# Gated linear attention and a top-2 expert router on one core: three leading experts instead of four, and one unit's routing moved into the attention chunks

## The chip, the cores and the metric

One core of a Trainium2 chip runs the whole program. The metric is device time in microseconds of one execution, as the median of repeated runs. The core has five engines that run their own instruction queues in order: PE (matrix products), DVE (vector work), ACT (scalar work, activations), POOL (here mainly indirect DMAs, which read or write rows by an index list) and SP (here plain DMAs and DMA transposes). They wait for each other through semaphores.

## The reference, cut to what matters

```python
# attention: batch 4, 8 heads, 768 steps, head width 48
state = np.zeros((B, H, D, D))
for t in range(S):
    state = alpha[:, :, t, :, None] * state + np.einsum('bhd,bhe->bhde', k[:, :, t], v[:, :, t])
    y[:, :, t] = np.einsum('bhd,bhde->bhe', q[:, :, t], state)
x = y.transpose(0, 2, 1, 3).reshape(3072, 384)
# router: 8 experts, hidden width 1024, two experts for a row
logits = x @ w_gate
noisy_logits = logits + np.log1p(np.exp(x @ w_noise)) * noise
top2 = np.argpartition(-noisy_logits, 2, axis=1)[:, :2]
top2_w = softmax of the two chosen logits
for e in range(8):
    for k in range(2):
        mask = top2[:, k] == e
        h = np.maximum(x[mask] @ w1[e], 0.0)
        out[mask] += top2_w[mask, k, None] * (h @ w2[e])
```

Everything is float32.

## The kernel before, in words

**Attention.** The 3,072 rows are worked on as 24 chunks of 128 (six chunks for a batch element). Within a loop step `n` PE transposes the inputs of chunks `n+2` and `n+3`, makes the output of chunk `n`, the state and the scores of chunk `n+1`, and brings the output of chunk `n-1` back to rows (`rows_of`, L277). DVE makes running products (two scans, L373 and L385), scales the queries (`q_P`, L413), adds the state (`S`, L472) and copies the scores under a mask (L445). The masked scores of a chunk are read by the product L254 of that chunk's output. The score tiles have one buffer each. The order of the pieces within a step is a list of names (`ORDER`, for the last but one step `LATE_ORDER`).

**Routing.** Six chunks make a unit; there are four units. `routing(u, on)` is a generator: logits, `Exp`, `Ln` on ACT (with loads of ACT's function tables), the best two of eight on DVE two chunks at a time (L742, L743), gates, ranks by two small matmuls (L795, L796), and the place of each row in a `table` in DRAM by expert. It leaves 12 indirect DMAs for each unit ("puts", L173) that POOL issues later, one or a few at a time (`put_some`). The units 0 and 1 are routed beside later attention chunks, at the steps and places of `ROUTE`; the units 2 and 3 beside the expert pairs, at the times in `beside()`. In the attention steps unit `u`'s pieces stand at `n - (u + 1) * UC + 1`, so they begin one step behind the unit's last chunk.

**Expert pairs.** The chosen rows are worked on in 24 pairs, each 256 rows of one expert, then three small tiles for what is left. A pair needs a list from the table (`tab`), its index list (`find_rows`, DVE), the gathered rows (`x_in`, POOL, L1008), their transposes, and the sums of weights and rows of a fast matrix scheme (DVE). `THIRD` is 4: pairs 0 to 3 are the first 256 rows of experts 0 to 3, pairs 4 to 15 three pairs each of experts 4 to 7, pairs 16 to 23 two each of experts 3 to 0. Pairs 0 and 1 have their layers one behind the other; from pair 2 on, the second layer of a pair lies between the steps of the next pair's first layer. Below `DEEP` (= `THIRD`) the first layer has 11 steps of four 128x128 products (`product1`, L1348), from `DEEP` on 10 (`step1`, L1356). The second layer has 7 steps (`product2`, L1363). Every matmul shows as two records, so a step has eight.

**Order.** Every step of a pair has a time on a plan in which pair `i` begins at `20 * i`; all steps are sorted by it and recorded in that order, and each engine runs its own in that order. The outputs of a pair go through one of two buffers (`os[i % 2]`, L1377 and L1381) and are written and added to `out` by indirect DMAs on POOL (L992 and L1000). `PUT_LATER` delays those of pairs 1 to 4 on the plan. ACT scales the first half of pair `i` into the buffer that pair `i-2` used, so it waits until that pair's DMAs have landed. A put of the table is also made to wait for the DVE sum that stands before it on the plan.

## Time and profile before

| | |
|---|---|
| median of 3 runs | 620.96 us (620.77 to 621.24) |
| the profiled execution | 621.97 us, of which the span from the first to the last instruction is 620.3 us |
| PE busy | 607.0 us, 98% of the span |
| DVE busy | 508.0 us, 82% |
| ACT busy | 330.9 us, 53% |
| POOL busy | 317.4 us, 51% |
| attention, to the first product of pair 0 | 0 to 153.7 us |
| pairs and small tiles on PE | 153.7 to 612.5 us |
| granted clock of PE | 0.997 of full speed |

PE is busy nearly all of the time, so a saving of work on another engine shows only where PE waits for it. Where PE waits, the view of waits names the engine and the line that ended the wait, and the timeline (instructions in order of time, with the idle time before each) shows when.

### The profile page before, as it was taken

What the parts mean: (1) busy time and instruction counts of PE and PEld (TensorE: products, weight loads), DVE (VectorE), ACT (ScalarE), POOL (GpSimd) and SP (SyncE); (2) the same over time, 40 slices, a digit from 0 to 9 for tenths busy, and PEclk for the clock granted to TensorE, in tenths of its full rate; (3) what the DMA queues carried; (4) which work ended last, traced back from release to release, by engine and by line L of the source; (5) the groups of instructions that cost most, each with busy time, mean ns of one, the idle gap of its engine ahead of it and who ended that gap; (6) DMA issues with size and microseconds to landing.
All of it is one profiled execution on the core that took longest, in us unless ns stands there. A gap on an engine that the chain in (4) does not pass through costs nothing.

```text
span 620.3 us, 14271 instructions
## 1 busy us (share of the span) xinstructions
PE 607.0 (98%) x5274; PEld 583.7 (94%) x5274; DVE 508.0 (82%) x1158; ACT 330.9 (53%) x665; POOL 317.4 (51%) x355
## 2 busy tenths in 40 slices
PE   8999999999999999999999999999999999999994
PEld 5899999999999999999999999999999999989894
DVE  8788898988879869968898798887688879878672
ACT  4877868685655334444444544445544445444431
POOL 7353267884137786545434434555347527443254
PEclk9999999999999999999999999999999999999998
DMA  9999999984997854664654837775997678885223
GB/s 144 175 199 223 237 188 175 214 179 106 259 235 145 235 136 128 126 166 121 115 126 105 171 66 200 193 98 132 271 211 199 140 184 221 181 220 118 80 44 55
DMA packets 181552, 101.09 MB, mean 163 GB/s; under 512 B 150088, under 2 KB 172074, under 8 KB 181472
## 3 DMA queue, kind: packets, MB, share of 16 engines
q1 hardware_dynamic: 145056, 35.56, 34.5%
q10 hardware_dynamic: 21280, 44.05, 24.4%
q0 software_dynamic: 15136, 20.47, 14.8%
q8 instruction: 44, 0.72, 0.5%
q14 instruction: 36, 0.29, 0.2%
HBM read 76.41 MB, written 24.22 MB: 162 GB/s over the span
## 4 chain that ended last, share of the span: by engine, by line
PE 81%; DVE 6%; POOL 5%; issue 4%; ACT 2%; DMA 1%; POOLq 0%; ACTq 0%; DVEq 0%
PE sc L1356 19%; PE h_ps L1363 18%; PE o_ps L1363 13%; PE c_ps L1356 8%; PE sc L1348 4%; PE tp L345 3%; PE sc L425 3%; PE y L254 2%; PE h_ps L277 2%; POOL table L173 2%; PE y L493 2%; DVE P_all L373 1%; POOL k_P L403 1%; PE tp L452 1%; PE h_half_ps L1678 1%
## 5 line engine op out<-in xcount | busy, mean ns | idle before, releaser
L992 POOL DMA_INDIRECT out_dram<-o,where x46 | 48.5, 1054 | 166.6 <-DVE o L1381 91.1
L1367 ACT ACTIVATE h<-h 128x512 f32<-128x512 f32 x92 | 56.9, 628 | 78.2 <-DVE h L1229 61.7
L1000 POOL DMA_INDIRECT out_dram<-o,where x44 | 71.0, 1615 | 13.4 <-issue 13.1
L1008 POOL DMA_INDIRECT x_in<-x_rows,where x48 | 58.6, 1220 | 24.4 <-issue 12.7
L1363 PE MATMUL o_ps<-wt,hx 128*128 128x192 f32 x384 | 70.8, 327 | 0.0
L1356 PE MATMUL sc<-yT,ws 128*128 128x128 f32 x480 | 66.6, 275 | 1.5 <-DVE m L1232 1.5
L1356 PEld LDWEIGHTS sc<-yT,ws 128*128 128x128 f32 x480 | 62.9, 191 | 1.8 <-DVE m L1232 1.8
L173 POOL DMA_INDIRECT table<-entry,place_u x48 | 55.0, 1145 | 16.5 <-issue 9.5
L1363 PEld LDWEIGHTS o_ps<-wt,hx 128*128 128x128 f32 x384 | 61.5, 190 | 1.8 <-issue 1.8
L403 POOL TENSOR_TENSOR k_P<-k_P,over 128x512 f32<-128x512 f32 (+1 forms) x24 | 27.7, 1154 | 40.5 <-DVE over L385 32.3
L1223 ACT COPY xt<-x_turned 128x768 uint16<-128x768 uint16 x44 | 43.8, 1053 | 2.1 <-DMA x_turned<-x_in 2.1
L345 PE MATMUL tp<-ident,ins 128*128 128x128 f32 x288 | 42.9, 282 | 1.6 <-ACT k_P L395 0.6
L1377 ACT ACTIVATE o<-h_ps,tab 128x192 f32<-128x192 f32 x46 | 19.4, 421 | 42.7 <-PE h_ps L1363 41.3
L345 PEld LDWEIGHTS tp<-ident,ins 128*128 128x128 f32 x288 | 32.1, 144 | 7.1 <-ACT k_P L395 1.0
L445 DVE COPY_PREDICATED shared<-upto,sc 128x512 f32<-128x512 uint32 x47 | 32.0, 736 | 7.6 <-PE sc L425 7.0
L1488 ACT COPY m<-sc 128x512 f32<-128x512 f32 x20 | 11.7, 586 | 48.0 <-PE sc L1356 48.0
L1363 PE MATMUL h_ps<-wt,h 128*128 128x192 f32 x192 | 35.2, 327 | 0.0
L1363 PE MATMUL o_ps<-w,h 128*128 128x192 f32 x192 | 35.2, 326 | 0.0
L1363 PE MATMUL h_ps<-wt,hx 128*128 128x192 f32 x192 | 35.2, 326 | 0.0
L1363 PE MATMUL h_ps<-w,h 128*128 128x192 f32 x192 | 35.1, 326 | 0.0
L1363 PE MATMUL h_ps<-w,hx 128*128 128x192 f32 x192 | 35.1, 326 | 0.0
L1356 PE MATMUL c_ps<-xs,w 128*128 128x128 f32 x240 | 33.3, 275 | 0.0
(333 smaller groups left out, 1611.9 us busy)
## 6 DMA issues: line engine op xcount, KB each, us to landing
w<-in_moe_w_dram ACTq DMA_DIRECT2D x33, 512.0 KB
w<-in_moe_w_dram ACTq DMA_DIRECT2D x44, 384.0 KB
ins<-in_alpha_dram SPq DMA_DIRECT2D x24, 192.0 KB
ins<-in_k_dram SPq DMA_DIRECT2D x24, 192.0 KB
ins<-in_q_dram SPq DMA_DIRECT2D x24, 192.0 KB
vt<-in_v_dram SPq DMA_DIRECT2D x24, 192.0 KB
x_rows<-y_sb SPq DMA_DIRECT2D x24, 192.0 KB
ins<-in_moe_w_dram ACTq DMA_DIRECT2D x9, 512.0 KB
```

The costliest lines, as they stand in the source:

```text
L173: put = nc.gpsimd.indirect_dma_start(out=table, out_offset=bass.IndirectOffsetOnAxis(ap=place, axis=0), in_=entry, in_offset=None, bounds_ ...
L345: nc.tensor.transpose(tp[:, j, :], src[:, 2 * j:2 * j + 2, :], ident)
L403: (nc.vector if n == NT - 1 else nc.gpsimd).tensor_tensor(c["k"][:, at], c["k"][:, at], over[:, at, 1:CB], op=ALU.mult)
L445: nc.vector.copy_predicated(MTs[n % 2][:, i], mask_upto, sc)
L992: put = nc.gpsimd.indirect_dma_start(out=out, out_offset=bass.IndirectOffsetOnAxis(ap=at, axis=0), in_=rows, in_offset=None, bounds_check= ...
L1000: add = nc.gpsimd.indirect_dma_start(out=out, out_offset=bass.IndirectOffsetOnAxis(ap=at, axis=0), in_=rows, in_offset=None, bounds_check= ...
L1008: nc.gpsimd.indirect_dma_start(out=rows, out_offset=None, in_=x_rows[0:units * UT, :], in_offset=bass.IndirectOffsetOnAxis(ap=at, axis=0), ...
L1223: nc.scalar.copy(halves[:, part], x_turned[:, :, part].rearrange("p s a t -> p s (a t)"))
L1348: nc.tensor.matmul(bank[name][:, f, :], W[:, ds(f * C, C)], X, start=new and f == 0, stop=True, skip_group_check=True)
L1356: nc.tensor.matmul(bank[name][:, 2 * h + f, :], W[h][:, ds(f * C, C)], X[h], start=new and not h and not f, stop=True, skip_group_check=True)
L1363: nc.tensor.matmul(bank[name], H[:, f, :], W[:, f, :], start=new and f == 0, stop=True, skip_group_check=True)
L1367: nc.scalar.activation(t, t if src is None else src, AF.Relu)
```

## The change

It changes numbers in the plan, and three conditions in the routing.

- `THIRD` becomes 3. Pairs 0 to 2 are the first rows of three experts, pairs 3 to 17 are five experts of three pairs each, pairs 18 to 23 two each of the first three. `DEEP` follows, so pair 3 has the 10-step first layer; the weights of an expert are loaded 11 times instead of 12.
- Unit 2 is routed at the steps `n` = 18 to 21 of the attention loop, by a third row of `ROUTE` that repeats the row of unit 1. Its rank and the check of expert lists (`check_third`, L859) use PSUM of the pool that the attention's rows use. Four of its puts stand in the attention loop, eight in pair 0.
- Unit 3 takes the times that unit 2 had in `beside()`, and its puts stand in pairs 1 and 2. The steps of the plan that follow from all lists (`route_on(3)` after the puts, `out_of_range`) come one pair sooner.
- `PUT_LATER` is empty: the outputs of pairs 1 to 4 are no longer delayed on the plan.
- The small tiles 0 and 1 begin at pairs 18 and 20 instead of 16 and 18; the third stays at 22.

```diff
-    AFTER_GROUP = (4, 5, 7)
-    THIRD = E - 4
+    AFTER_GROUP = (5, 6, 7)
+    THIRD = E - 5
...
-            for u in range(2):
+            for u in range(NU - 1):
                 for _ in range(ROUTE[u].count((n - (u + 1) * UC + 1, place))):
                     next(routes[u], None)
...
-            if (u, c) in ((NU - 2, 2), (NU - 1, 0)):
+            if (u, c) == (NU - 1, 0):
                 nc.scalar.activation(unread_exp, ones[0:1, 0:1], AF.Exp)
...
-        if u < NU - 2:
+        if u < NU - 1:
             nc.scalar.activation(unread_exp, ones[0:1, 0:1], AF.Exp)
...
-        rank = few(on, [C, UC, E], "rank", u >= NU - 2)
+        rank = few(on, [C, UC, E], "rank", u >= NU - 1)
...
-    DEEP, BY_DMA = THIRD, THIRD - 2
+    DEEP, BY_DMA = THIRD, THIRD - 1
...
-        PUT_LATER = {1: 13.0, 2: 16.0, 3: 12.0, 4: 6.0}
+        PUT_LATER = {}
...
-            left += [(t, lambda: route_on(2)) for t in when((0, 8.95), (0, 12.0), ...
-            left += [(t, lambda: route_on(3)) for t in when((1, 5.0), (1, 10.2), ...
+            left += [(t, lambda: route_on(3)) for t in when((0, 8.95), (0, 12.0), ...
```

Where instructions then stand:

DVE in loop step 20, between the scaled queries of chunk 22 (`q_P`) and the masked scores of chunk 21. Before:

```order
L413 TENSOR_TENSOR q_P<-tp,P_all 128x512
L472 TENSOR_TENSOR S_156<-S_155,o_ps 128x192
L445 COPY_PREDICATED shared<-upto,sc_2352 128x512
L445 COPY_PREDICATED shared<-upto,sc_2353 128x512
L1182 TENSOR_SCALAR tab_2279<-tab_2279 128x2
```

Now (the two chunks of `top` and `at` that stand behind `q_P` here stand twice more in the rows above it):

```order
L413 TENSOR_TENSOR q_P<-tp,P_all 128x512
L742 MAX top<-noisy 128x8
L743 MAX_INDEX at<-top,noisy 128x8
...
L749 CAST at_f<-at 128x6x2
L754 TENSOR_TENSOR entry<-top 128x12
L766 TENSOR_TENSOR den<-entry 128x6
...
L783 TENSOR_TENSOR counts<-picked 128x6x8
L788 SCALAR_TENSOR_TENSOR past<-within,counts 128x56
L472 TENSOR_TENSOR S_156<-S_155,o_ps 128x192
L445 COPY_PREDICATED shared<-upto,sc_2396 128x512
L445 COPY_PREDICATED shared<-upto,sc_2397 128x512
```

Unit 2's choice of experts now stands ahead of the state and the masked scores of chunk 21; `den` waits for ACT's gates.

ACT in loop step 19, between the state block of chunk 19 and the output `yT` of that chunk. Before:

```order
L454 COPY k_end<-tp 128x512
L415 COPY P_end<-P_all 128x4
L479 COPY S_block<-S 64x4x48 x2
L496 COPY yT<-y 128x512
L363 ACTIVATE ins,above<-ins,less 128x8x48
```

Now:

```order
L479 COPY S_block<-S 64x4x48 x2
L689 ACT_TABLE_LOAD
L689 ACTIVATE noisy<-noisy 128x48
L496 COPY yT<-y 128x512
L363 ACTIVATE ins,above<-ins,less 128x8x48
```

A load of the function table and the `Ln` of unit 2 now stand between them; DVE's next instruction of unit 2 needs that `Ln`.

POOL from the gather of pair 4 to the outputs of pair 1. Before:

```order
L1008 DMA x_in<-x_rows,where_2781 128x768 x2
L173 DMA table<-entry,place_u 25600x8
L753 MEMSET entry 128x12x4
...
L173 DMA table<-entry,place_u 25600x8 x6
L1008 DMA x_in<-x_rows,where_3175 128x768 x2
...
L992 DMA out_dram<-o_186,where_2463 3072x384
L1000 DMA out_dram<-o_186,where_2463 3072x384
```

Now:

```order
L1008 DMA x_in<-x_rows,where_3051 128x768 x2
L173 DMA table<-entry,place_u 25600x8 x2
L992 DMA out_dram<-o_186,where_2520 3072x384
L1000 DMA out_dram<-o_186,where_2520 3072x384
...
L1155 DMA tab_3225<-table 128x6x8
L1008 DMA x_in<-x_rows,where_3279 128x768 x2
```

Two table puts stand ahead of the outputs of pair 1 there, where nine and the gather of pair 5 stood.

## Rows read from the trace of the kernel before

**Rows 1.** Waits of PE: engine, line, waited for, total us, times, longest.

```profile
PE sc L1356 <- DVE m L1232: 1.5, 1, 1.5
PE tp L345 <- DVE q_P L413: 0.4, 2, 0.2
```

**Rows 2.** Windows, pairs 0 to 3: length, then busy us of PE, PEld, DVE, ACT, POOL.

```profile
152.20:224.00 71.80, 71.80 (x573) 71.49 (x574) 61.55 (x188) 38.94 (x70) 37.70 (x45) 1.00 0.87 215
```

**Rows 3.** Timeline, DVE, unit 1's routing: start, duration, line, op, [idle before <-releaser].

```profile
97.24 0.21 DVE L737 TENSOR_TENSOR noisy<-noisy,noise 128x48 f32<-128x48 f32 x1
...
97.95 1.36 DVE L445 COPY_PREDICATED shared<-upto,sc 128x512 f32<-128x512 uint32 x2 [0.19 <-PE sc L425]
...
99.89 1.21 DVE L373 TENSOR_TENSOR_SCAN P_all<-shared,least 128x516 f32<-128x516 f32 x1
...
104.57 0.28 DVE L749 CAST at_f<-at 128x12 f32<-128x12 uint32 x1
...
106.76 0.33 DVE L472 TENSOR_TENSOR S<-S,o_ps 128x192 f32<-128x192 f32 x1
```

**Rows 4.** Timeline, ACT: unit 1's `Ln`, and the state block of chunk 19.

```profile
95.67 1.28 ACT L689 ACT_TABLE_LOAD   x1
96.97 0.24 ACT L689 ACTIVATE noisy<-noisy 128x48 f32<-128x48 f32 x1
...
134.09 0.71 ACT L479 COPY S_block<-S 64x192 f32<-64x192 f32 x2 [1.70 <-POOL S L473]
```

**Rows 5.** Timeline, DVE, chunks 20 to 23 of the attention.

```profile
135.54 1.37 DVE L445 COPY_PREDICATED shared<-upto,sc 128x512 f32<-128x512 uint32 x2 [0.62 <-issue]
136.79 2.02 DVE L373 TENSOR_TENSOR_SCAN P_all<-shared,least 128x516 f32<-128x516 f32 x1
...
141.37 0.35 DVE L472 TENSOR_TENSOR S<-S,o_ps 128x192 f32<-128x192 f32 x1 [0.43 <-PE o_ps L467]
142.35 1.35 DVE L445 COPY_PREDICATED shared<-upto,sc 128x512 f32<-128x512 uint32 x2 [0.62 <-PE sc L425]
...
149.12 0.68 DVE L413 TENSOR_TENSOR q_P<-tp,P_all 128x512 f32<-128x512 f32 x1
```

**Rows 6.** Timeline, DVE, the places of unit 2's rows and what follows.

```profile
180.46 0.26 DVE L801 TENSOR_TENSOR picked<-picked,rank 128x96 f32<-128x96 f32 x1
...
181.56 0.25 DVE L722 TENSOR_TENSOR lg<-lgs 128x96 f32<-128x96 f32 x1
```

**Rows 7.** Timeline, PE: chunk 22's output; the rank of unit 3 and what follows.

```profile
149.98 1.09 PE L254 MATMUL y<-shared,vt 128*48 128x128 f32 x16
...
201.99 0.34 PE L795 MATMUL rank<-counts,before 128*128 128x48 f32 x2
...
202.37 1.53 PE L1363 MATMUL o_ps<-wt,hx 128*128 128x192 f32 x8
```

**Rows 8.** Timeline, PE: second layers of pairs 3 and 4, then two later pairs.

```profile
225.97 1.47 PE L1363 MATMUL o_ps<-w,h 128*128 128x192 f32 x8
...
246.28 1.47 PE L1363 MATMUL o_ps<-w,h 128*128 128x192 f32 x8
...
390.10 0.61 PE L1356 MATMUL sc<-xt,w 128*128 128x128 f32 x4
...
390.99 1.47 PE L1363 MATMUL o_ps<-w,h 128*128 128x192 f32 x8
...
409.02 1.47 PE L1363 MATMUL o_ps<-w,h 128*128 128x192 f32 x8
```

**Rows 9.** Timeline, ACT: pair 3's first half scaled into its output buffer.

```profile
230.97 0.42 ACT L1377 ACTIVATE o<-o_ps,tab 128x192 f32<-128x192 f32 x1 [3.86 <-DMA out_dram<-o,where]
```

**Rows 10.** Timeline, SP and ACT: the DMA transposes of pair 2, and their readers.

```profile
165.37 2.82 SPq L1212 DMA_TRANSPOSE x_turned<-x_in  x2
...
178.75 1.06 ACT L1223 COPY xt<-x_turned 128x768 uint16<-128x768 uint16 x1
...
455.92 1.07 ACT L1223 COPY xt<-x_turned 128x768 uint16<-128x768 uint16 x1 [2.12 <-DMA x_turned<-x_in]
```

## What the change was predicted to do

> **What bounds the kernel now.** I read the page first: PE is busy for 98% of the span, so the time is PE's own work plus its few waits. Then the waits of PE, by line. The longest that belong to this change's neighbourhood are small: one of 1.5 us for a sum of weights, and two of 0.2 us in the attention chunks, one behind the routing of unit 0 and one behind that of unit 1 [rows 1]. The windows say the same of the first four pairs: PE busy 71.80 us of 71.80, DVE only 61.55 [rows 2]. So DVE, ACT and POOL may be relieved in these pairs without any gain; only PE's work counts, and what makes PE wait. The timelines then give four places: the last attention chunks, where DVE is full [rows 5]; the few PE instructions that vanish [rows 7, 8]; one wait on ACT for outputs [rows 9]; and the DMA transposes of pair 2 [rows 10].
>
> **Part 1, unit 2's routing in the attention chunks: +4.0 us.** The masked scores of chunk 22 must stand before PE can make that chunk's output. On DVE they end when `q_P` of the next chunk starts, at 149.12 [rows 5]; PE begins the output at 149.98 [rows 7], 0.86 later, after work of its own. So there is 0.86 us of slack at that place, and what DVE loses above it PE waits for.
>
> What DVE gets to do between chunks 20 and 23 is priced by what unit 1 took, and by unit 2's own rows in the pairs.
> - Start: ACT's state block of chunk 19 begins at 134.09 and takes 0.71 [rows 4]. Behind it stand the table load and the `Ln`. For unit 1 the `Ln` began 1.30 after the load (95.67 to 96.97) and took 0.24 [rows 4]. So the noisy logits can begin on DVE at 134.09 + 0.71 + 1.30 + 0.24 = 136.34, where DVE before began its masked copy at 135.54 [rows 5]: 0.80 late.
> - Two operations that finish the noisy logits: 97.24 to 97.95 less the wait of 0.19, 0.52 [rows 3].
> - `top` and `at` for six chunks, two at a time: from 97.95 to 99.89 a masked copy and one pair of chunks lie, 1.94 [rows 3]; the copy alone is 1.25 (135.54 to 136.79) [rows 5], so 0.69 for two chunks, 2.07 for six.
> - Gates and counts: 104.57 to 106.76, 2.19 [rows 3].
> - Places from the rank: 180.46 to 181.56, 1.10 [rows 6].
>
> Together 0.52 + 2.07 + 2.19 + 1.10 = 5.88, and 0.80 for the start. Against it go waits in which DVE now has work: 0.43 and 0.62 [rows 5], and the scan of 2.02 [rows 5], which took 1.21 beside unit 1 [rows 3]: I estimate that it does so again, since POOL's vector work, which ran beside it, stands elsewhere now; 0.81. That is 1.86 in all. `q_P` of chunk 23 starts at 149.12 + 0.80 + 5.88 - 1.86 = 153.94, and PE's output of chunk 22 at about 154.0 instead of 149.98: **+4.0**. All that stands behind moves with it, pair 0 too. If the scan stays at 2.02 it is 4.8; if the late start is covered by the first wait, 3.2. The rank's matmuls and ACT's gates lie within this stretch of DVE and are not counted again. The puts that POOL issues here hide behind the chunks, as those of unit 1 did; without that cover, a put would hold only the gathers, which are rival 2.
>
> What this relieves in the pairs, DVE's routing of unit 2, is worth nothing there, since PE did not wait [rows 2].
>
> **Part 2, PE's own work in the pairs.** The rank of a unit takes PE from 201.99 to 202.37, 0.38 [rows 7]. Unit 2's now lies in the attention, where PE waits for DVE anyway: **-0.38**. Pair 3 loses one step of four products; a step lasts 0.89 (390.10 to 390.99) [rows 8]: **-0.89**. The one load of an expert's weights that is saved, with its sums on DVE, hides behind PE now (PE has no idle time there [rows 2]): 0. The most it could be worth is the one wait for such a sum, 1.5 [rows 1], which lies elsewhere and has pairs in front of it that stay as they are.
>
> **Part 3, outputs of pair 1.** ACT waits 3.86 us before it can scale pair 3's first half, for the DMAs that write pair 1's outputs [rows 9]. PE feels it: from the second layer of pair 3 to that of pair 4 it takes 20.31 us (225.97 to 246.28), where a regular pair takes 18.03 (390.99 to 409.02) [rows 8]. The difference is 2.28. In the new order two table puts stand ahead of these outputs on POOL, where nine and a gather stood, so they go out well before they are needed: **-2.28**. What is late next in the pair is PE itself, as in the regular pairs.
>
> **Part 4, the rest: 0.** Unit 3's routing and its puts take the times that unit 2's had, with the same distance to the lists that need them and with DVE less filled. The small tiles and the plan's other steps come a pair or two sooner with the same instructions; their cover is PE at 71.80 of 71.80 [rows 2], and a small tile that came too soon would cost about the wait that such a piece has now, 1.5 [rows 1].
>
> **The sum.** 4.0 - 0.38 - 0.89 - 2.28 = +0.45 us on the profiled execution of 621.97, so 622.42. That execution lies 1.01 above the median of 620.96, so I add the 0.45 to the median: **621.4 us**. With the ends of part 1 (3.2 and 4.8) its own range is 620.6 to 622.2.
>
> **Rival 1, faster: DVE has room.** Units 0 and 1 were routed the same way, and PE waited 0.2 us behind each [rows 1]. If unit 2's work also fits into DVE's gaps, only the 0.80 of the late `Ln` stays, and the sum is 0.80 - 0.38 - 0.89 - 2.28 = -2.75: 618.2. For it speaks that the operations are the same. Against it, that around chunk 20 to 22 DVE's own waits are only 0.43 and 0.62 [rows 5], too few for 5.88, and that for unit 1 there were many more chunks left over which PE could fall behind and catch up, while behind unit 2 stand three. Chance 0.15.
>
> **Rival 2, slower: the transposes of pair 2 come late.** Pair 2's rows are gathered by POOL, and SP turns them by DMA (issued 165.37 for 2.82; ACT reads them at 178.75) [rows 10]. Between gathers and outputs POOL has seven more items there than before: unit 2's puts in pair 0 and more. From the end of the second issue (168.19) to the reader there are 10.6 us. Both ends move by about 4.0 with part 1, but the issue by about 1 more for the puts. The one reader in the trace that had to wait for such a transpose waited 2.12 [rows 10]. If it happens to pair 2, ACT's queue stands, and PE behind it: 0.45 + 2.12 = 2.57, so 623.5. It decides from a landing later than about 9.5 us after the second issue. Against it, no other reader of the trace waits so. Chance 0.13.
>
> **Rival 3, the change does not do what it says.** POOL's outputs of pair 1 now stand ahead of the puts of unit 3, but they come only when the pair's results do, and if the DMAs in front (gathers, puts with their waits) still hold POOL, ACT's wait of rows 9 stays and the 2.28 are not gained: 623.7. [Rows 9] show only that the outputs landed late, not which item held them. Chance 0.08.
>
> **Rival 4, the table load costs more than its row.** In this trace the `Ln` begins 1.30 after the load starts, and the load lasts 1.28 [rows 4]; nothing else lies between. Were the load followed by as long again, 1.28, before the `Ln` could run, DVE's chain would start 1.3 later and the time would be 622.7. The rows of unit 1 show no such gap, so its chance is 0.04. The Trainium skill ("ScalarE: Activation LUTs", section "What ACT_TABLE_LOAD costs") says that a switch costs a drain of about 1380 ns beside the load of about 1283 ns; by that figure, an estimate from the page, the sum would be about 622.8. The load agrees with the trace, the drain does not show in it.
>
> **How the numbers follow.** Forecast 0.60, rivals 0.15, 0.13, 0.08, 0.04. About 0.2%, 619.7 to 622.2, is what a measurement of this kernel can tell from no change. Of the forecast's 0.60 I put 0.48 within its own range, which lies within that bound, 0.02 below it and 0.10 above, since the terms I left at 0 in part 4 are more likely to cost than to gain. Faster: 0.15 + 0.02 = 0.17. Same: 0.48. Slower: 0.10 + 0.13 + 0.08 + 0.04 = 0.35. The range goes from 619.5 to 623.9: it takes in the forecast and rivals 2 to 4 and leaves out rival 1 (0.15) and what lies beyond 623.9, some 0.04.
>
> **What would show it.** Part 1: the first product of pair 0 at about 157.7 instead of 153.7; DVE with hardly an idle moment from 136.3 to `q_P` of chunk 23; PE waiting for DVE in the chunks 21 to 23. If pair 0 starts before 155.5, rival 1 has it. Part 2: pair 3 in steps of L1356, and no rank between the layers of pairs 0 to 2 but unit 3's. Part 3: no wait for `out_dram` at L1377, and some 18 us from pair 3's second layer to pair 4's. Rival 2: a wait for `x_turned` at L1223 in pair 2. Rival 4: the `Ln` 2.6 instead of 1.3 behind its load. The prediction is wrong if PE has new idle time in pairs 0 to 5, or if the shift of pair 0 lies outside 3.2 to 4.8.

## The result: slower by 1.1%, and the profile after

The changed kernel takes 627.96 us in the median of 6 executions (623.91 to 632.24), the kernel before 620.99 (6 executions, 620.40 to 621.63). The ratio is 1.0109, with a 95% interval of 1.0067 to 1.0151, so some 7 us more. The forecast was 621.4, the range 619.5 to 623.9: the time lies outside it. Two things are new: the shift of the pairs is larger than forecast, and the times scatter over 8 us, where the kernel before stays within 1.3. In some runs below the kernel before took 630 to 633 us as well; there only the difference to it counts.

The profiled execution took 628.84 us, 6.87 more than that of before. It is one of six that lie 8 us apart, so the table shows where this execution lost its time, and not where each of them did. It is read from PE's timeline: for each pair the start of its second layer, and its distance to the one before it.

| stretch on PE | before, us | after, us | difference |
|---|---|---|---|
| start to pair 0's first product | 153.69 | 159.23 | +5.54 |
| to pair 0's second layer | 13.50 | 14.32 | +0.82 |
| to that of pair 1 | 19.37 | 23.68 | +4.31 |
| to that of pair 2 | 20.49 | 19.82 | -0.67 |
| to that of pair 3 | 18.93 | 18.03 | -0.90 |
| to that of pair 4 | 20.31 | 18.26 | -2.05 |
| to that of pair 13 | 162.74 | 162.52 | -0.22 |
| to that of pair 20 | 134.22 | 135.59 | +1.37 |
| to PE's end | 69.28 | 69.28 | 0.00 |
| from PE's end to the span's end | 7.80 | 6.50 | -1.30 |

The span grows from 620.3 to 627.2. The table's rows sum to 6.9.

PE's waits in the changed kernel, as [rows 1] show them for before (engine, line, what was waited for, us in total, times, longest):

```profile
PE sc L1348 <- ACT m L1423: 2.4, 1, 2.4
PE h_ps L277 <- ACT yT L496: 1.4, 2, 1.0
...
PE h_ps L795 <- DVE counts L783: 1.3, 1, 1.3
PE sc L1356 <- ACT m L1496: 0.6, 1, 0.6
```

The first is in pair 1 and the last in pair 18; the two in the middle are in the attention's end. The one wait of 1.5 us in [rows 1] is gone, and these took its place.

**The attention's end.** DVE's timeline, which answers [rows 5] (start, duration, line, [idle before]):

```profile
136.45 1.39 DVE L737 TENSOR_TENSOR noisy<-noisy,noise 128x48 f32<-128x48 f32 x1 [1.48 <-ACT noisy L689]
137.87 0.42 DVE L738 TENSOR_TENSOR noisy<-noisy,lg 128x48 f32<-128x48 f32 x1
138.22 1.35 DVE L445 COPY_PREDICATED shared<-upto,sc 128x512 f32<-128x512 uint32 x2
...
140.14 1.21 DVE L373 TENSOR_TENSOR_SCAN P_all<-shared,least 128x516 f32<-128x516 f32 x1
...
144.89 0.18 DVE L749 CAST at_f<-at 128x12 f32<-128x12 uint32 x1
...
147.33 0.33 DVE L472 TENSOR_TENSOR S<-S,o_ps 128x192 f32<-128x192 f32 x1
...
155.44 0.68 DVE L413 TENSOR_TENSOR q_P<-tp,P_all 128x512 f32<-128x512 f32 x1
```

`q_P` of chunk 23 starts at 155.44, forecast was 153.94, before 149.12. The `Ln` is not to blame: its load and itself on ACT, then the POOL product beside DVE's first row, and the same product before the change, where it stood beside the scan of 2.02 in [rows 5]:

```profile
134.88 1.28 ACT L689 ACT_TABLE_LOAD   x1
136.17 0.24 ACT L689 ACTIVATE noisy<-noisy 128x48 f32<-128x48 f32 x1
```

```profile
136.57 1.20 POOL L403 TENSOR_TENSOR k_P<-k_P,over 128x512 f32<-128x512 f32 x1
```

```profile
136.50 1.21 POOL L403 TENSOR_TENSOR k_P<-k_P,over 128x512 f32<-128x512 f32 x1
```

PE in the same place, then in pair 1:

```profile
147.09 0.62 PE L795 MATMUL h_ps<-counts,before 128*128 128x48 f32 x2 [1.27 <-DVE counts L783]
...
147.94 2.03 PE L493 MATMUL y<-q_P,S_block 128*128 128x128 f32 x8
...
155.37 1.25 PE L254 MATMUL y<-shared,vt 128*48 128x128 f32 x16
...
159.23 1.07 PE L1348 MATMUL sc<-xt,w 128*128 128x128 f32 x8
...
186.61 1.12 PE L1348 MATMUL sc<-xt,ws 128*128 128x128 f32 x8
190.14 1.16 PE L1348 MATMUL sc<-xs,ws 128*128 128x128 f32 x8 [2.41 <-ACT m L1423]
191.13 1.55 PE L1348 MATMUL sc<-xt,w 128*128 128x128 f32 x8
192.48 1.91 PE L1348 MATMUL c_ps<-xt,w 128*128 128x128 f32 x8
...
197.23 1.47 PE L1363 MATMUL o_ps<-w,h 128*128 128x192 f32 x8
```

The output of chunk 22 is at 155.37 (forecast 154.0, before 149.98 in [rows 7]). A product that takes 1.06 elsewhere takes 2.03 at 147.94 and up to 1.91 behind the wait of pair 1. The windows say why (length, then busy us of PE, PEld, DVE, ACT and POOL, the granted clock, the busy share of the DMA engines and GB/s):

```profile
148.00:149.00 1.00, 1.00 (x6) 1.00 (x6) 0.96 (x4) 0.70 (x2) 0.25 (x1) 0.50 0.52 183
192.00:193.00 1.00, 1.00 (x7) 1.00 (x6) 0.21 (x1) 0.00 (x0) 0.65 (x1) 0.50 1.05 389
```

A granted clock of 0.50 is the 1.2 GHz level. It stands behind both of PE's longer idle stretches (1.02 and 1.27 us close together, and 2.41).

**Pair 1.** ACT's reader of pair 2's transposes, SP's issues of them, and POOL ahead of these; they answer [rows 10]:

```profile
188.60 1.04 ACT L1223 COPY xt<-x_turned 128x768 uint16<-128x768 uint16 x1 [3.38 <-DMA x_turned<-x_in]
```

```profile
174.11 4.27 SPq L1212 DMA_TRANSPOSE x_turned<-x_in  x2
```

```profile
168.03 1.37 POOL L173 DMA_INDIRECT table<-entry,place_u  x1 [1.85 <-DVE ws L1232]
169.70 1.63 POOL L1008 DMA_INDIRECT x_in<-x_rows,where  x1 [0.30 <-issue]
171.63 1.02 POOL L1008 DMA_INDIRECT x_in<-x_rows,where  x1 [0.30 <-issue]
```

ACT waits 3.38 us for the transposes, and copies the first layer's sum that PE needs (L1423) only behind that. Counted from pair 0's first product, the two transposes are issued from 14.9 to 19.2 us, before the change from 11.7 to 14.5.

**Pairs 3 to 4.** [Rows 9] has no counterpart: no L1377 of pair 3 waits for `out_dram`. The second layers, against [rows 8]:

```profile
235.08 1.47 PE L1363 MATMUL o_ps<-w,h 128*128 128x192 f32 x8
...
253.34 1.47 PE L1363 MATMUL o_ps<-w,h 128*128 128x192 f32 x8
```

18.26 us instead of 20.31.

### The profile page after: what moved, and what is told of

The parts are those of the page before. It is cut to its first block, busy times and chain, and to the rows that moved or that the text cites. A ratio compares the mean times of both kernels' runs of the same rounds, so it can differ in the third digit from the quotient of the medians.

```text
span 627.2 us, 14224 instructions
## 1 busy us (share of the span) xinstructions
PE 611.4 (97%) x5266; PEld 586.7 (94%) x5266; DVE 505.8 (81%) x1144; ACT 331.2 (53%) x667; POOL 316.4 (50%) x357
## 4 chain that ended last, share of the span: by engine, by line
PE 77%; DVE 8%; DMA 5%; ACT 3%; issue 3%; POOL 2%; ACTq 1%; POOLq 0%; DVEq 0%; SPq 0%
PE sc L1356 20%; PE h_ps L1363 17%; PE o_ps L1363 13%; PE c_ps L1356 8%; DMA x_turned<-x_in 4%; PE tp L345 3%; PE sc L1348 3%; PE sc L425 2%; PE h_ps L277 2%; PE y L254 2%; DVE P_all L373 2%; DVE over L385 1%; DVE shared L445 1%; PE y L493 1%; DMA x_in<-x_rows,where 1%
## 5 line engine op out<-in xcount | busy, mean ns | idle before, releaser
L1356 PE MATMUL sc<-yT,ws 128*128 128x128 f32 x504 | 69.8, 275 | 0.0
L1356 PEld LDWEIGHTS sc<-yT,ws 128*128 128x128 f32 x504 | 66.1, 192 | 0.0
L173 POOL DMA_INDIRECT table<-entry,place_u x48 | 54.3, 1131 | 20.8 <-issue 14.5
L403 POOL TENSOR_TENSOR k_P<-k_P,over 128x512 f32<-128x512 f32 (+1 forms) x24 | 27.7, 1155 | 43.9 <-DVE over L385 30.9
L1377 ACT ACTIVATE o<-h_ps,tab 128x192 f32<-128x192 f32 x46 | 19.4, 421 | 39.6 <-PE h_ps L1363 35.6
L1356 PE MATMUL c_ps<-xs,w 128*128 128x128 f32 x252 | 35.0, 275 | 0.0
```

The lines of the kernel that those rows point to most:

```text
L173: put = nc.gpsimd.indirect_dma_start(out=table, out_offset=bass.IndirectOffsetOnAxis(ap=place, axis=0), in_=entry, in_offset=None, bounds_ ...
L403: (nc.vector if n == NT - 1 else nc.gpsimd).tensor_tensor(c["k"][:, at], c["k"][:, at], over[:, at, 1:CB], op=ALU.mult)
L1356: nc.tensor.matmul(bank[name][:, 2 * h + f, :], W[h][:, ds(f * C, C)], X[h], start=new and not h and not f, stop=True, skip_group_check=True)
L1377: nc.scalar.activation(sums(i, s)[:, half], bank[name], AF.Copy, scale=gate(i, s))
```

## The experiments

Unless said otherwise the edit is made in the changed kernel. Times are medians beside that of the kernel before on the same chip.

### Part 3 alone, in the kernel before

```diff
-        PUT_LATER = {1: 13.0, 2: 16.0, 3: 12.0, 4: 6.0}
+        PUT_LATER = {}
```

> The kernel before with one part of the change alone: the outputs of pairs 1 to 4 no longer put later on the plan. Theory: ACT's wait of 3.86 us for pair 1's output buffer goes, pair 3 to 4 takes 18.0 to 18.3 us instead of 20.31, and the time falls by about 2.2 us, to 618.8. Rival: the outputs now stand ahead of the gathers and puts of units 2 and 3 on POOL and make these late; then a wait for x_turned or for a list of the table comes in pairs 3 to 6 and the time is 621 or more.

Measured: 618.28 against 620.92, ratio 0.9961 (0.9946 to 0.9975). Second layers of pairs 3 and 4:

```profile
225.98 1.47 PE L1363 MATMUL o_ps<-w,h 128*128 128x192 f32 x8
244.02 1.47 PE L1363 MATMUL o_ps<-w,h 128*128 128x192 f32 x8
```

18.04 us, and no reader of transposes waits anywhere in this profile. Part 3 needs none of the rest, and this version beats both kernels.

### What DVE work in the last chunks costs

In the kernel before, `N` instructions are added in loop step 20 ahead of the state of chunk 21, 15 in one run and 30 in the other:

```diff
+                if n == 20:
+                    chunk.insert(9, lambda: [nc.vector.max(out=spare, in_=ones) for k in range(N)])
```

> The kernel before with 15 more DVE instructions (the best eight of 128 constants, estimated at 0.2 us each from the rows of 0.15 to 0.17 us on 8 to 48 elements, 3.0 us in all) ahead of the state of chunk 21, where the change put the choice of unit 2's experts; nothing else is moved. Theory (DVE has 1.05 us of waits and PE 0.86 us of slack there, and past these what DVE loses PE waits for): of 3.0 us some 1.9 are covered, pair 0 begins about 1.1 us later, at 154.8, and the time is 622.1. Rival (the work fits into gaps): pair 0 at 153.7, 621.0.

> The same with 30 instructions, 6.0 us. Theory: the 3.0 us more over the run with 15 come through in full, pair 0 begins at about 157.8, and the time is about 625.1; a granted clock of 0.5 for some microseconds behind PE's wait, as in the changed kernel, may stand there and cost nothing, or may add to it. Rival: pair 0 below 155.5 and the time below 622.5.

Measured: 634.38 and 640.45 beside 630.31, so +4.1 (ratio 1.0069, 1.0049 to 1.0090) and +10.1 (1.0164, 1.0120 to 1.0207). The instructions took longer than I had estimated:

```profile
140.88 4.89 DVE L1849 MAX8 spare<-ones 128x8 f32<-128x128 f32 x15
145.69 0.34 DVE L472 TENSOR_TENSOR S<-S,o_ps 128x192 f32<-128x192 f32 x1
```

```profile
147.61 2.33 PE L254 MATMUL y<-shared,vt 128*48 128x128 f32 x15 [2.71 <-DVE shared L445]
```

They take DVE 4.81 us (140.88 to 145.69), and pair 0 begins at 158.08, 4.39 late. The 30 take 9.75 us (141.31 to 151.06), and pair 0 begins at 163.36, 9.67 late. From 15 to 30 DVE has 4.94 us more, and pair 0 begins 5.28 later, 0.43 of it because the 30 were reached that much later. So what is added once the gaps are filled comes through one for one. That is the mechanism of part 1.

How much of the first 4.81 us was covered is harder to see, because PE's clock falls behind its wait (0.50 from 148 to 150 us). The output of chunk 21 and the scores behind it, with 15 instructions and in the kernel before:

```profile
150.91 1.16 PE L425 MATMUL sc<-q_P,k_P 48*128 48x128 f32 x16
```

```profile
145.04 1.09 PE L254 MATMUL y<-shared,vt 128*48 128x128 f32 x16
...
146.51 1.16 PE L425 MATMUL sc<-q_P,k_P 48*128 48x128 f32 x16
```

From L254 to L425 it is 3.30 us (147.61 to 150.91) instead of 1.47: PE comes to L254 2.57 late and loses 1.83 more at the slow clock, and it waits for nothing from there to pair 0. DVE by itself was less late:

```profile
148.05 1.22 DVE L373 TENSOR_TENSOR_SCAN P_all<-shared,least 128x516 f32<-128x516 f32 x1
```

Before, this scan began at 144.14, so it is 3.91 late: 0.9 of the 4.81 went into DVE's waits of 0.43 and 0.62 [rows 5]. Less PE's slack of 0.86 at the output of chunk 22, pair 0 would have begun some 3.0 us late at full clock, an estimate from these rows. The cover of 1.9 that I had expected is then about right (4.81 less 3.0 is 1.8), and the slow clock hid it. The edit also moved six short instructions of DVE (L1183 to L1198) ahead of the masked scores of chunk 21, where they take 0.89 us (145.94 to 146.83).

### The clock behind PE's wait

```diff
+        if u == NU - 2:
+            for k in range(8):
+                nc.tensor.matmul(rank, before, within[:, :, 0:UC].rearrange("p e c -> p c e"), start=True, stop=True)
```

> The changed kernel with eight small matmuls on constants ahead of the rank of unit 2 on PE, where PE waits 1.27 us for the counts; their result is overwritten. In the changed kernel the granted clock falls to 0.50 behind that wait, and the state product of chunk 21 takes 2.03 us instead of 1.06. Theory (DVE, not PE, sets the end of the attention): the clock stays higher, the product takes about 1.1, and pair 0 still begins at 159.0 to 159.4. Rival (the slow clock is a part of the 1.5 us by which the shift exceeds 4.0): pair 0 begins at 157.7 to 158.4.

Measured, one execution: 623.00. PE stays busy in that wait, the product of chunk 21 is quick again, and the clock of that microsecond is 1.00:

```profile
147.88 1.12 PE L493 MATMUL y<-q_P,S_block 128*128 128x128 f32 x8
...
159.28 1.07 PE L1351 MATMUL sc<-xt,w 128*128 128x128 f32 x8
```

```profile
148.00:149.00 1.00, 1.00 (x10) 0.88 (x10) 1.00 (x3) 0.66 (x2) 0.29 (x1) 1.00 0.53 196
```

Pair 0 begins at 159.28, with the slow clock at 159.23: the slow clock lies under DVE's chain. It need not be the added products that kept the clock up, for it also stayed in the run without the wait for the sum (below), where PE has the same waits of 1.02 and 1.27 us:

```profile
147.06 0.44 PE L795 MATMUL h_ps<-counts,before 128*128 128x48 f32 x2 [1.27 <-DVE counts L783]
...
147.70 1.12 PE L493 MATMUL y<-q_P,S_block 128*128 128x128 f32 x8
```

Pair 0 begins at 159.21 there. The slow clock can cost something all the same: in the run with the gather first (below) it lasts longer, DVE waits 1.11 us for scores that PE makes slowly, and pair 0 begins at 160.43.

```profile
158.94 1.36 DVE L445 COPY_PREDICATED shared<-upto,sc 128x512 f32<-128x512 uint32 x2 [1.11 <-PE sc L425]
```

### The two products of the noisy logits, later

```diff
-((1, 9), (2, 8), (2, 11), (2, 13), (3, 4), ...
+((1, 9), (2, 8), (2, 13), (2, 13), (3, 4), ...
```

> The changed kernel with one piece of unit 2's routing (the two products that finish the noisy logits on DVE) two places later in the attention step, behind the masked scores. In the changed kernel DVE waits 1.48 us for the Ln there and the first of the two products takes 1.39 us instead of 0.21 beside a POOL product. If these two are the reason that the shift of pair 0 is 5.5 instead of 4.0 us, the masked scores begin at 135.5 again, the scan behind them takes 2.0, and pair 0 begins 1.0 to 1.5 us sooner, at about 158. If POOL's product only stretches another DVE instruction by as much, it begins at 158.4 or later. The time follows by as much (about 627), but for the wait of pair 1 that this leaves alone.

Measured: 622.56 beside 620.92 (1.0041, 1.0020 to 1.0061). DVE:

```profile
135.33 1.35 DVE L445 COPY_PREDICATED shared<-upto,sc 128x512 f32<-128x512 uint32 x2 [0.62 <-issue]
136.58 0.99 DVE L737 TENSOR_TENSOR noisy<-noisy,noise 128x48 f32<-128x48 f32 x1
137.61 0.42 DVE L738 TENSOR_TENSOR noisy<-noisy,lg 128x48 f32<-128x48 f32 x1
```

The masked copy fills the wait for the `Ln`, `q_P` of chunk 23 starts at 154.05 instead of 155.44, and pair 0 at 158.01 instead of 159.23. The product is still stretched, to 0.99, but less: it began 0.29 behind the POOL product (136.29) and ended with it. The time fell by more than this 1.2 because pair 1 had no wait in this run's profile, which the edit does not explain; see the transposes.

### The gather of pair 2

First its place among the puts, then the wait of the puts:

```diff
-            puts = when((0, 0.5), (0, 2.0), (0, 3.5), (0, 5.0), (0, 6.5), (0, 8.0), ...
+            puts = when((0, 5.0), (0, 5.6), (0, 6.3), (0, 7.0), (0, 7.7), (0, 8.4), ...
```

```diff
-            left += [(t, lambda: put_some(1, latest["sum"])) for t in puts]
+            left += [(t, lambda t=t: put_some(1, None if t < T else latest["sum"])) for t in puts]
```

> The changed kernel with three of unit 2's table puts moved from ahead of the gather of pair 2 to behind it on POOL; nothing else. Theory A (the puts, one of which waits for a sum of weights, hold that gather; the DMA transposes of pair 2 are then issued too late): the second issue of the transposes comes some 5 us sooner against pair 0's first product, ACT's wait for x_turned (3.38 us in the changed kernel's profile) is gone or below 0.5, PE has no wait in pair 1, and no half clock behind it; from the second layer of pair 0 to that of pair 1 it takes 19.4 us as before the change instead of 23.7, and the time falls by about 4 us, to 624. Theory B (the transposes are slow because of the other transfers in flight, whenever they are issued): the wait stays at 2 to 4 us and the time at 627 to 629. Both: pair 0 still begins at 159.2.

> The changed kernel with the eight puts of pair 0 no longer made to wait for the DVE sum that stands ahead of them on the plan; their order on POOL stays. If the put's wait for the sum (1.85 us on POOL) alone makes the gather late, the gather of pair 2 comes 1.6 us sooner, and ACT's wait for x_turned falls from 3.4 to about 1.8, PE's from 2.4 to about 0.8, perhaps with no half clock behind it: 625 to 626. If the number of puts ahead of the gather counts (1.3 us each), the wait is nearly as before and the time stays at 627 to 628.

Measured: 625.03 (622.48 to 627.53) and 624.50 (623.46 to 625.92) beside 620.92. In both PE takes 19.4 to 19.7 us to pair 1's second layer instead of 23.68. With the gather first ACT waits for nothing there, and without the sum's wait 0.98 us. But the first still scatters over 5 us: in its profile ACT waits 5.97 us for transposes at 539, and pair 20 takes 22.52 us instead of 19.66.

Then the counter-test, in the kernel before:

```diff
+                if (i, s) == (BY_DMA, 0):
+                    tc.add_manual_dep(get.ins, latest["sum"].name, AFTER, reason="a later gather")
```

> The kernel before with one wait added on POOL: the gather of pair 2 is issued only behind DVE's first sum of pair 0's hidden rows, which in the trace ends 10.3 us after pair 0's first product; until now it is issued 5.7 us after it, and in the changed kernel 10.5. Nothing else is changed. Theory (the gather's place alone makes the transposes late): the second transpose is issued some 4.5 us later, ACT waits for x_turned in pair 2 for 1 to 4 us where it waited for nothing, PE waits up to 2.5 us and runs at half clock for some us behind it, and the time is 621 to 626 with a scatter of 4 us or more where it was about 1. Rival (the gather is early enough either way, and the changed kernel's late transposes come from the puts in flight): no wait at x_turned above 0.5, 621.0, scatter 1.

Measured: 620.94 beside 621.00 (0.9998, 0.9989 to 1.0008), ten executions from 620.37 to 621.76. The gather went out even later than I wanted:

```profile
165.26 1.00 POOL L1008 DMA_INDIRECT x_in<-x_rows,where  x1 [11.76 <-ACT h L1369]
```

Nobody waits for these transposes. So the gather's place alone does not cost anything here, and the theory as I put it falls.

### Puts out of flight, and pair 3 in pair 2's place

The gather stays late, but the five puts behind it go behind the gather of pair 3:

```diff
-            puts = when((0, 0.5), (0, 2.0), (0, 3.5), (0, 5.0), (0, 6.5), (0, 8.0), (0, 9.5), (0, 11.0), ...
+            puts = when((0, 0.5), (0, 2.0), (0, 3.5), (1, 7.6), (1, 7.7), (1, 7.8), (1, 7.9), (1, 8.0), ...
```

> The changed kernel with the gather of pair 2 as late as it is there (three puts of pair 0 stay ahead of it), but the five puts behind it, which in the changed kernel are issued while pair 2's transposes move, 20 us later on the plan, behind the gather of pair 3. Theory A (puts in flight make the stream of the transposes long, 10 to 11 us instead of 6 to 8, and that with the late start is what PE waits for): the stream takes 6 to 8 us, no wait at x_turned in pair 2 above 0.5, 622.5 to 623.5 and a scatter of 2 us, as with a late gather in the kernel before. Theory B (long and short streams come in the changed kernel whatever the puts do): the wait is there in some executions, the times scatter over 5 us or more from 623 to 632.

> The kernel of the run with five puts out of flight a second time, since its first run fell on disturbed executions (the kernel before took 632 us beside it). Theory A (puts in flight make the transposes' stream long): stream of 6 to 8 us, no wait at x_turned in pair 2 above 0.5, 622.5 to 623.5, scatter 2 us. Theory B (the stream is long or short whatever the puts do): a wait of 2 to 4 us at x_turned in some executions, a scatter of 5 us or more between 623 and 632.

Measured: the first time 648.95 beside 632.68, with executions from 641.21 to 890.30, nothing to conclude; the second time 629.94 beside 620.36 (1.0153, 1.0115 to 1.0190), which neither theory had: the executions lie from 628.51 to 632.42, theory A said 622.5 to 623.5, and theory B's wait of 2 to 4 us in pair 2 is not there. In its profile pair 2's reader waits 0.62 us and PE for nothing in pair 1; but two puts now stand ahead of the gather of pair 3, which goes out at 193.34 instead of 190.28, and pair 3's reader is late:

```profile
208.04 1.95 ACT L1223 COPY xt<-x_turned 128x768 uint16<-128x768 uint16 x2 [4.62 <-DMA x_turned<-x_in]
```

```profile
211.43 3.78 PE L1348 MATMUL sc<-xs,w 128*128 128x128 f32 x16 [4.49 <-DVE h L1232]
```

The second line also shows the half clock, 3.78 us for what takes 1.95. From pair 1 to pair 2 PE takes 26.78 us instead of 19.82. The loss has moved to the next pair and grown.

### How long the transposes take

From the packets of SP's queue: the first and the last of the 1,536 packets of 256 bytes that the two transposes of pair 2 make, in us from pair 0's first product. "Fill" is the run with the added products, "products later" that with the noisy logits moved.

| kernel | second issue done | first packet | last | length | ACT's wait | PE to pair 1 |
|---|---|---|---|---|---|---|
| before | 14.5 | 13.0 | 23.9 | 11.0 | 0 | 19.37 |
| before, gather late | 21.3 | 18.8 | 24.5 | 5.7 | 0 | 19.37 |
| changed | 19.2 | 18.3 | 28.6 | 10.2 | 3.4 | 23.68 |
| tile loads later | 19.2 | 18.2 | 27.7 | 9.5 | 2.7 | 23.02 |
| fill | 18.8 | 17.6 | 25.4 | 7.7 | 0.1 | 19.37 |
| products later | 19.3 | 18.7 | 25.4 | 6.7 | 0 | 19.37 |
| puts out, second run | 19.0 | 18.2 | 26.4 | 8.2 | 0.6 | 19.37 |
| no sum wait | 16.1 | 15.5 | 25.8 | 10.4 | 1.0 | 19.67 |
| gather first | 14.4 | 14.1 | 19.5 | 5.4 | 0 | 19.37 |
| all four edits | 14.7 | 14.4 | 17.9 | 3.5 | 0 | 19.37 |

The packets take 3.5 to 11.0 us, with the same work. Where the last one comes at 25.8 or later, ACT waits; at 25.4 it waits 0.1 at most. So it takes a late start and a long stream together: before the change the stream was long and hidden (the last packet at 23.9, ACT's read at 25.1 [rows 10]); the change takes some 5 us of start away. What makes a stream long stays open. Puts in flight are not needed for it (before has none there), nor are they enough (all four edits has 46 of their packets in the shortest stream). A rival that no run tests is the loading of weights from ACT's queue: 20 and 59 of its packets of 4 KB fall into the two shortest streams, 174 to 191 into those of 5.7 to 8.2 us, 210 to 236 into the four longest. But a longer stream also meets more of them, so the count by itself shows no cause.

### Small tiles and leading experts

```diff
-(-67.9, -66.5, -65.1) if j == 0 else (-49.4, -48.4, -47.4)
+(-67.9, -66.5, -65.1) if j == 0 else (-49.4, -48.4, -47.4) if j == 1 else (-33.4, -32.4, -31.4)
```

> The changed kernel with the three early weight loads of the third small tile 16 us later on the plan, so that they no longer leave beside those of the second tile's second layer and pair 20's transposes. If the small tiles' nearness makes the transposes of pairs 20 and 21 land late, the waits for x_turned between 510 and 560 us (2.1 us in the changed kernel, 6.0 with the gather first) are gone, pairs 17 to 20 lose at most what the wait near 500 us costs, and the runs scatter less: about 627, lowest to highest within 4 us. If not, 628 as before, with a scatter of 8 us.

Measured: 624.34, but from 622.51 to 632.22 in nine executions (without the two longest, to 629.36), beside 621.01. The wait near 540 us is down to 0.30 and pairs 17 to 20 lose 0.2 at most, but that near 500 us (2.51) and that of pair 2 are there. The third tile's loads are not what makes the times scatter.

```diff
-    AFTER_GROUP = (5, 6, 7)
-    THIRD = E - 5
+    AFTER_GROUP = (4, 5, 7)
+    THIRD = E - 4
...
-    DEEP, BY_DMA = THIRD, THIRD - 1
+    DEEP, BY_DMA = THIRD, THIRD - 2
```

> The changed kernel with four leading experts again, small tiles at pairs 16, 18 and 22 with it; unit 2 stays routed in the attention chunks, the times of unit 3 and the puts stay. Theory: pair 0 begins at 159.2 and ACT waits for the transposes of pair 2 as in the changed kernel, pair 3 has 11 steps (+0.89), but the waits near 500 and 540 us and what they cost PE (1.35 us) are gone: 627.5, and the scatter is smaller. Rival (three leading experts have no part in the late waits): the waits near 500 us are there, and 628.9.

Measured: 633.61 (630.45 to 640.20) beside 621.01. The times of the plan no longer fit: PE waits 1.6 us for a sum of weights on DVE in pair 4 and 1.3 for another sum of DVE in pair 11. It is inconclusive on the late transposes, but the one reader that waits here, at 464 us, waits only 0.5.

The change without its part 1: the kernel before with `THIRD = E - 5`, the new small tiles, `PUT_LATER = {}`, and

```diff
+            left += [(t, lambda: route_on(3)) for t in when((1, 5.0), (1, 10.2), (1, 18.0), (1, 19.2), (2, 1.0), (2, 1.1), (2, 5.2), (2, 8.2), (2, 10.5))]
```

> The change without its part 1: unit 2 is routed beside pairs 0 and 1 again, at the times that it had before, and unit 3 in pairs 1 and 2, its puts done by the middle of pair 3; three leading experts, the small tiles and the undelayed outputs are as in the changed kernel. Theory (the DVE work in the last attention chunks and what it pushes is all that the change costs; parts 2 and 3 give what was reckoned): pair 0 begins at 153.7, pair 3 has one step fewer (0.89), pairs 3 to 4 take 18 us, pair 1 20.0 or less, and the time is 620.96 - 0.89 - 2.64 (the measured worth of the undelayed outputs) = 617.4. Rival (three leading experts make the rest late: lists that all units fill are needed 20 us sooner, small tiles lie closer together): waits for x_turned or for a list of the table in pairs 3 to 6, or 1 to 3 us lost around pairs 17 to 20, and 619 to 621.

Measured: 628.78 beside 621.01 (1.0125, 1.0101 to 1.0150). Pair 0 begins at 153.36 and pair 3 has one step fewer, as expected. But pair 2 takes 29.03 us. DVE waits for pair 4's list, whose puts have just gone out, and behind it in DVE's queue stand sums that PE needs:

```profile
204.66 0.17 DVE L1182 TENSOR_SCALAR tab<-tab 128x2 f32<-128x2 f32 x1 [5.30 <-DMA tab<-table]
```

ACT stood 4.19 us for gates of unit 3 besides. These are my times in the plan, and others might do better. With three leading experts the lists of all units are needed 20 us sooner on the plan; that the routing in the chunks is the way to have them is argued from this wait, and not shown.

### All four edits together

The gather first, no wait for the sum, the products later, the third tile's loads later.

> The changed kernel with four edits at once: the gather of pair 2 ahead of pair 0's puts, these puts with no wait for a sum of weights, the two products of the noisy logits behind the masked scores, and the third small tile's early weights later. Theory (the change's loss is the DVE work in the attention, 4.3 us with the products moved, and late transposes; the rest gives what was reckoned): pair 0 at 158.0, no wait for x_turned in pair 2, PE without waits from pair 0 to the end but for some tenths, and 621.5 to 622.5 with a scatter below 3 us. Rival (something else makes transposes late): waits for x_turned above 2 us that PE feels, a median of 624 or more, a scatter of 5 us or more.

> The kernel of the run with all four edits a second time, since in its first run all kernels, the one before too, were some 9 us longer, with idle engines in pairs 1 and 2 that wait for nothing the profile shows. Theory as there: pair 0 at 158.0, no wait for x_turned that PE feels, 621.5 to 622.5 where the kernel before has 621.0, scatter below 3 us. Rival: waits for x_turned near 500 and 540 us that PE feels, 624 or more, scatter of 5 us or more.

Measured: the first time 638.20 beside 630.31 (1.0110, 1.0071 to 1.0149), with a wait of 3.72 us on PE in pair 0 and idle stretches in pair 2 that wait for nothing shown; the second time 622.50 beside 621.00 (1.0032, 1.0011 to 1.0052), nine of ten executions from 621.81 to 623.07 and one of 628.21. Pair 0 begins at 158.01 and no reader of transposes waits in the profile. So this is the change without late transposes, and it is still slower than before by 1.5 us. In its profile PE ends 2.0 us later than before (614.52 against 612.53): 4.3 of shift and 0.86 in pair 0, against 0.89 for the step, 2.06 for the outputs and 0.2 for pair 2. What follows PE's end is 1.8 shorter there, but that stretch takes 5.9 to 7.8 us in these profiles whatever the edit.

## Why the prediction was wrong, by its own steps

The forecast was +0.45 for the profiled execution, and it took 6.9 more in its span. Of the 6.45 between them 1.54 are in part 1, 4.31 in rival 2, which the sum had left out, 0.82 in pair 0 and 1.37 in pairs 13 to 20, both put at nothing; behind PE's end 1.3 came back, and parts 2 and 3 with the rest gave 0.3 more than forecast. Both signs that the prediction named for being wrong are there: pair 0 shifts by 5.54, outside 3.2 to 4.8, and PE has new idle time in pairs 0 and 1.

**What bounds the kernel: right.** PE has the time, DVE sets the attention's end. With 4.94 us more on DVE there, pair 0 began 5.28 later.

**Part 1: right in mechanism, 1.5 us too small.** Its terms, forecast and measured: late start 0.80 and 0.91; the two products 0.52 and 1.77 (136.45 to 138.22); `top` and `at` 2.07 and 2.16; gates and counts 2.19 and 2.44; places 1.10 and 1.10. Together 6.68 and 8.38; the filled waits and the shorter scan gave back 1.86 and 2.06. The failed term is the products, 1.25 of the 1.50, and with it the reason for dropping the scan's stretch of 0.81, that POOL's vector work stands elsewhere now. The scan did fall to 1.21, but POOL's product of `k_P` was still there (136.57, before 136.50), and now it stood beside a DVE instruction of 0.21 us [rows 3], which took 1.39. [Rows 5] held the hint: the scan is long where POOL multiplies. The Trainium skill has the rule ("SBUF — State Buffer", section "SBUF: two separate sides"): a GpSimd instruction that reads SBUF and a DVE instruction with two SBUF inputs hold a shared port pair one at a time, and the one that starts second is blocked for the whole of the other. The trace agrees on the blocking: L737 ends at 137.84, just behind POOL's product (136.57 to 137.77), and in the run with the products later at 137.57, behind one that ends at 137.49. It does not agree on the order: L737's row starts 0.12 ahead of POOL's in the first case, and POOL's product is no longer for it. By that rule I should have moved the stretch, not dropped it.

**Rival 1, DVE has room:** no. Pair 0 began 5.5 us late, not 0.8.

**Part 2: right.** Pair 3's step gave 0.90 for 0.89. Pair 2 gave 0.67 for 0.38; the check of the lists, which I left out, moved with the rank (its product is now at the attention's end).

**Part 3: right.** 2.05 for 2.28 in the change; alone 2.27 in the trace (20.31 to 18.04) and 2.64 in the medians.

**Rival 2: it happened in the profiled execution, with a chance of 0.13, and its price was twice mine.** The step that failed is "the issue by about 1 more for the puts". Between the gathers of pairs 1 and 2 five puts stand, 1.3 to 1.7 us each with the gap behind it, and one of them first waits 1.85 for a sum that waits for weights; the second transpose ended its issue 4.7 us later against pair 0, not 1. I had counted the items and not walked POOL's queue. The threshold of 9.5 us behind the second issue was then down to 6.8 (178.38 to 185.2, when ACT was free). The price was 2.12 in the forecast; it is 4.31: PE waits 2.41, and the half clock behind it makes 7.09 us (190.14 to 197.23) of what took 5.36 before (181.19 to 186.55), 1.73 more. It does not happen each time: with the same puts ahead of the gather ACT waits 2.7 us in the run with the tile loads later, and 0.1 or nothing in those with the fill and with the products later, whose edits touch neither gather nor transposes. What makes the difference, the length of the stream, stays open.

**Rival 3 and rival 4:** neither. The outputs came in time, and the `Ln` began 1.29 us behind its load.

**Part 4: wrong at 0.** Pairs 13 to 20 lose 1.37 us, 1.30 of it in pair 18, to transposes that land late near 500 us:

```profile
501.13 1.05 ACT L1223 COPY xt<-x_turned 128x768 uint16<-128x768 uint16 x1 [4.42 <-DMA x_turned<-x_in]
```

```profile
503.89 0.71 PE L1356 MATMUL sc<-xt,q_P 128*128 128x128 f32 x4 [0.59 <-ACT m L1496]
```

In the kernel before a reader waited 2.12 at 456 us [rows 10], which PE did not feel. In the run with all edits 0.2 of the loss is left, in three others nothing, in the one with the gather first 2.9; its cause is not settled. Pair 0's 0.82 was not in the sum at all; DVE's sums there wait 2.02 us for weights, and PE has two short waits; why these weights come late is not shown. The 1.3 us gained behind PE's end were not foreseen; that stretch differs by as much between runs.

## What to carry to other kernels

A move onto an engine that is nearly full is paid one for one as soon as its short waits are filled (here 8.4 us of work and delay met 2.1 us of cover on DVE), and the stretch that two engines' instructions give each other moves along with the order: price it where the new neighbours meet. Of what is moved onto an issuing queue, walk the queue in the new order with its waits, up to the next transfer that somebody needs, and where PE then stands as long as here (2.4 us), add the slow clock behind it (1.7) to the price. And try the parts of a change alone: here one line of it is worth 2.6 us, and the rest of it costs 4 to 10 (622.50 and 627.96 against 618.28).

## What the runs showed of the hardware

The DMA transposes of one pair, the same 1,536 packets of 256 bytes, took 3.5 to 11.0 us in the runs of the table. Waits of 1.0 and 1.3 us on PE, 1.6 us apart, were followed by a granted clock of 0.50 for some 3 us in the changed kernel, as one wait of 2.41 was. The same two waits were not followed by it in the run without the wait for the sum, nor was one idle stretch of 1.5 us in the kernel before (231.8 to 233.4).
